# Routing steps of a fused attention and mixture-of-experts kernel put in another order, and one weight split moved by a turn

## The chip, the cores and the metric

The kernel runs on one core of one Trainium2 chip. What counts is the time of one execution on the device in microseconds (us). Before the change three runs took 968.52, 968.83 and 969.94 us; the median is 968.83 us. The engines are named as in the profile: PE is the matrix engine, DVE the vector engine, ACT the scalar engine, POOL the general engine that here also issues the scattering DMAs, and SP the engine that issues the other DMAs.

## The reference

Local attention over chunks of 64 tokens feeds a mixture of experts. Cut to what matters:

```python
# attention: 8 heads, q and k scaled inputs, chunks of 64 tokens
scores = (q_c @ k_c.T) / sqrt(64);  scores -= scores.max(-1)
attn = exp(scores);  attn /= attn.sum(-1) + 1e-9
x = (attn @ v_c)                      # to rows: 4608 tokens x 512
# gate: two of eight experts for each token
noisy = x @ w_gate + log1p(exp(x @ w_noise)) * noise
top2 = the two largest of the 8;  l = noisy[top2] - max
w = exp(l) / (sum(exp(l)) + 1e-9)
# experts: 512 -> 1024 -> 512
for e in range(8):
    for k in range(2):
        mask = top2[:, k] == e
        out[mask] += w[mask, k] * (relu(x[mask] @ w1[e]) @ w2[e])
```

## The kernel before

The 4608 tokens are 36 tiles of 128. The function `attend(it)` is one turn of a software pipeline written out by hand: in turn `it` PE computes the scores of tile it+1 (L443), the product with V of tile it-2 (`pv`, L472), the transposes of the probabilities (L460) and of the finished rows (L488). DVE takes the maxima (L448), subtracts them (L453), and in `norm_c` (L483) divides the product with V by the row sums and writes the rows x. `pv` has a single pair of PSUM banks, so `pv` of the next tile cannot begin before `norm_c` of the last one has read them. Each engine runs its instructions in program order; an instruction that waits holds up all behind it on its engine.

The rows x lie in a ring of buffers, `rows = ...tile_pool(name="rows", bufs=5)` (L339), each holding four tiles. Every fourth turn `x_next` (L438) takes the next buffer with a small memset on DVE, and that memset must wait until the rows of the group five buffers back have been scattered.

Routing runs beside the attention. After four tiles the gate matmul (L500), its transposes (L510) and a sum (L517) give the logits of a *group* of four tiles. There are seven such groups, 0 to 6, and a last one with eight tiles. The generator `route(g)` then computes, on ACT and DVE, the noisy logits (L541 to L549), the eight sorted values of each token (`MAX`, L555), the indices (L559), two one-hot tables (`goh`, L563) and their sum (`gohb`, L567). PE turns these into ranks by small matmuls (L577, L579: the *rank matmuls*). From the ranks and a running count `run` DVE makes `gr`, `gohr` and the slot numbers `lii` (L596 to L610). Beside that stand the weights of the two experts: the difference of the two maxima `gex` (L570), its exponential (L581), the sum `gsm` (L587), its reciprocal (L590) and the second weight (L607). The code of the token (L584) is written into the row.

The generator yields the name of the engine that its next step uses, and `attend` advances it at fixed places: three DVE steps after the subtraction (ahead of `norm_c`) and three after `norm_c` in each turn. A yield of "dve" costs one of these six steps; what stands between two yields goes as one step. A "pe" step is done in a fixed place in PE's row, and a "wait" holds the group until the next turn.

When a group has its slot numbers, eight scatters (four tiles, two experts each) go to a list. `scatter` takes from this list, once after the maxima and once ahead of `norm_c` in each turn: two spacing memsets (L640), a one-element copy (L642) that keeps POOL from running ahead, and an indirect DMA (L644) that writes 128 rows of x to their slots in DRAM.

Meanwhile W1 of expert 0 is split for the later three-pass matmuls: `w_split` makes a high part on ACT (L88) and a low part on POOL (L89), one half of a 128-row chunk a turn, in turns 7 to 14.

After the attention the expert blocks follow. `layer1` and `layer2` consist of matmuls at L239 from there to the end, and the rows are added into the output by indirect DMAs (L206).

Of the kernel before, what the change touches and what calls it, by code (L numbers as in the profile page):

```python
# [13 lines left out]
AF = mybir.ActivationFunctionType  # L14
# [35 lines left out]
def kernel(ctx, tc, qT, kT, vh, wgn, noise, w1, w2, out, caps=CAPS):  # L50
    nc = tc.nc
# [15 lines left out]
    def w_load(e, which, c):  # L67
        st = stage.tile([P, 1024], FT, name="st")
        staged[e, which, c] = st
        if which == 1:  # L70
            if e == 0:
                nc.sync.dma_start(st, w1[0, c * P:(c + 1) * P, :])
            else:
                for j in range(4):
                    nc.sync.dma_start(st[32 * j:32 * j + 32], w1v[ds(place[e], 1), c, j].rearrange("o r f -> (o r) f"))
        else:
            nc.sync.dma_start(st.rearrange("p (f n) -> p f n", f=2),
                              w2[ds(place[e], 1) if e else slice(0, 1), 2 * c * P:(2 * c + 2) * P, :]
                              .rearrange("o (f p) n -> p (o f) n", f=2))
# [270 lines left out]
    def load_qk(j):  # L350
        if j < NT // 2:
            QB[j] = loads.tile([P, 2, 4, P], FT, name="qb", bufs=RING)
            for h in range(2):
                nc.sync.dma_start(QB[j][h::2], qT[HALF[h], 2 * j:2 * j + 2])
                nc.sync.dma_start(KB[j % RING][h::2, h], kT[HALF[h], 2 * j:2 * j + 2])

    def load_v(j):
        if j < NT // 2:
            for h in range(2):
                nc.sync.dma_start(VB[j % RING][h::2, h], vh[HALF[h], 2 * j:2 * j + 2])  # L360
# [79 lines left out]
    def scores(t):  # L440
        for hp in range(4):
            for q in HALF:
                nc.tensor.matmul(PS[q, t % 2, hp * P:(hp + 1) * P], QB[t // 2][:, t % 2, hp, q],  # L443
                                 KB[t // 2 % RING][:, :, t % 2, hp, q], start=True, stop=True)
# [13 lines left out]
    def p_trans(t):  # L458
        for hp in range(4):
            nc.tensor.transpose(PS[:, 2, hp * P:(hp + 1) * P], PR[t][:, hp * P:(hp + 1) * P], ident)  # L460
# [37 lines left out]
    def gate_mm(g):  # L498
        for d in range(ND):
            nc.tensor.matmul(PS[32 * d:32 * d + 32, 6, :], wg[:, d, :], XT[g][:, d], start=True, stop=True)  # L500
# [19 lines left out]
    def route(g):  # L520

        V = nc.vector
# [27 lines left out]
        m = gate.tile(n8, FT, name="gm")  # L550
# [15 lines left out]
        V.memset(ohb[:, G], 0.0)  # L566
        V.tensor_add(ohb[:, 0:G], oh[:, 0], oh[:, 1])  # L567
        ex, sm = nm("gex"), nm("gsm")
        yield "dve"
        V.tensor_sub(ex, m[:, :, 1], m[:, :, 0])  # L570
        if g == LAST:
            yield "wait"
            yield "wait"
# [3 lines left out]
        nc.tensor.matmul(rk, before, ohb, start=True, stop=False)  # L577
        for k in range(1, G + 1):
            nc.tensor.matmul(rk[:, k:G + 1], ones, ohb[:, 0:G + 1 - k], start=False, stop=(k == G))  # L579
        yield "act"  # L580
        nc.scalar.activation(ex, ex, AF.Exp)  # L581
        for x, s in parts:
            yield "dve"
            V.scalar_tensor_tensor(x.bitcast(I32)[:, :, CODE], mi[:, s, 0], 8192.0, tok[:, ts][:, s], op0=OP.mult, op1=OP.add)  # L584
        yield "wait"
        yield "dve"
        V.tensor_scalar(sm, ex, 1.0, 1e-9, op0=OP.add, op1=OP.add)  # L587
# [6 lines left out]
        yield "dve"  # L594
        r8 = n3("gr8")
        V.scalar_tensor_tensor(r8, rk[:, 0:G], 8.0, be(run8), op0=OP.mult, op1=OP.add)  # L596
        yield "dve"
        V.scalar_tensor_tensor(run8, rk[:, G], 8.0, run8, op0=OP.mult, op1=OP.add)
        yield "dve"
        ohr = gate.tile([P, 2, G, NE], FT, name="gohr")  # L600
# [65 lines left out]
    def load_early():  # L666
        for i, js, m in early:
            gather(i)
            early_loads.append(nc.sync.dma_start(
                meta0[i], by_slot[js * P:(js + m) * P, 0, CODE:USED].rearrange("(j p) c -> p j c", p=P)))  # L670
        early.clear()
# [28 lines left out]
    def next_turn():  # L700
        for r in routing:
            if r[1] == "wait":
                r[1] = next(r[0])
# [22 lines left out]
    def attend(it):  # L726
        STEPS = 6
        if it % 2:
            load_qk((it - 1) // 2 + 3)
        if it % 2 == 0 and it >= 4:  # L730
            load_v((it - 4) // 2 + 3)
            if it == 32:
                load_early()
        if it in (9, 11):
            for r in range(CLEAN + 64 * (it // 2 - 4), CLEAN + 64 * (it // 2 - 3), 16):
                nc.sync.dma_start(slots[r * NE:(r + 16) * NE, 0:USED], zero)
        if it == 11:
            nc.sync.dma_start(slots[(CLEAN + P) * NE:NLIST * P * NE, CODE:USED].rearrange("(p r) c -> p r c", p=P),
                              zero[:, 0:3 * (NLIST * P - CLEAN - P) // 16].rearrange("p (r c) -> p r c", c=3))
        if it in range(4, 8):  # L740
            w_load(0, 1, it - 4)
        if it in (29, 31, 33, 35):
            w_load(0, 2, (it - 29) // 2)
        next_turn()
        if it == 0:
            scores(0)
        if it <= 1:
            p_trans(0) if it else scores(1)
        if it == 2:
            pv(0)  # L750
        if 0 < it < NT - 1:
            scores(it + 1)
        if 0 < it - 2 < NT:
            pv(it - 2)
        gated = it - 4 >= 0 and (it - 4) % 4 == 3
        if gated:
            gate_mm((it - 4) // 4)
        if 0 < it - 1 < NT:
            p_trans(it - 1)
        if 0 <= it - 3 < NT:  # L760
            x_trans(it - 3)
        if it - 5 >= 0 and (it - 5) % 4 == 3:
            gate_turn((it - 5) // 4)
            if grp_of[it - 5] != grp_of.get(it - 4):
                r = route(grp_of[it - 5])
                routing.append([r, next(r)])
        step_route("pe")
        if 0 <= it - 2 < NT:
            norm_a(it - 2)
        if 0 <= it - 1 < NT:  # L770
            p_copy(it - 1)
        if it < NT:
            mx = soft_max(it)
            soft_sub(it, mx)
            scatter(1, mx[0:1, 0, 0:1])
            soft_exp(it)
        if 0 <= it - 3 < NT:
            x_copy(it - 3)
        if gated:
            gate_copy((it - 4) // 4)  # L780
        step_route("dve", STEPS // 2)
        if 0 <= it - 2 < NT:
            norm_b(it - 2)
            scatter(1, RC[it - 2][0:1, 0, 0])
            norm_c(it - 2)
        if it - 5 >= 0 and (it - 5) % 4 == 3:
            gate_sum((it - 5) // 4)
        step_route("act")
        step_route("dve", STEPS // 2)
        if it >= 1 and (it - 1) % 4 == 0:  # L790
            x_next((it - 1) // 4)
        if it in range(33, 38):
            zero_out(3)
        if it == NT + 2:
            scatter(2, XT[(it - 3) // 4][0:1, 0, (it - 3) % 4, 0:1])
        elif it == NT + 3:
            scatter(2, LS[(it - 4) // 4][0:1, 0, 0:1])
        if it in range(7, 15):
            w_split(0, 1, *wq.pop(0), eng=nc.gpsimd)

    for it in range(NT):
# [242 lines left out]
```

## Time and profile before

| | |
|---|---|
| median of three runs | 968.83 us |
| profiled execution | 974.74 us |
| its span in the trace | 972.9 us |
| PE busy | 951.2 us, 98% |
| DVE busy | 457.5 us, 47% |
| ACT busy | 287.3 us, 30% |
| POOL busy | 236.3 us, 24% |

A row of a timeline gives start, duration, engine, line, operation, output<-input and, in brackets, how long the engine sat idle before it and what ended that idle time. Runs of equal instructions are one row with a count (x16). A row of windows gives, for a stretch of time, the busy time and the number of instructions of PE, PE's weight loads, DVE, ACT and POOL, then the granted clock of PE (1.00 is full), the share of the DMA engines that was busy, and GB/s.

The turns are easily found in the trace: each begins on DVE with L448. Turn 13 begins at 50.10 us, turn 14 at 53.37, turn 26 at 94.31, turn 30 at 110.13. The expert blocks begin at 137.53 us.

### The profile page before, as it was taken

To read this page: it belongs to the slowest core of one execution; us is meant where nothing else is said; L and a number is where in the kernel's file an instruction comes from. 1 tells how busy PE (TensorE), PEld (TensorE's weight loads), DVE (VectorE), ACT (ScalarE), POOL (GpSimd) and SP (SyncE) were. 2 spreads that over 40 slices of the span, in tenths; PEclk is the share of its full clock that TensorE was granted. 3 is DMA by queue.
4 is the path that set the end of the run, shared out by engine and by line. 5 is a ranking of instruction groups with operands and counts; after the bars stand their busy time and mean duration, and the time that the engine had idled before them with its cause. 6 is when DMAs were issued, how large, how long until landed. Compare 5 with 4: busy or idle time off the path is not lost. (4 is left out here: it accounts for less than half of the span.)

```text
span 972.9 us, 16180 instructions
## 1 busy us (share of the span) xinstructions
PE 951.2 (98%) x5776; PEld 846.5 (87%) x5776; DVE 457.5 (47%) x1026; ACT 287.3 (30%) x623; POOL 236.3 (24%) x426
## 2 busy tenths in 40 slices
PE   7999899999999999999999999999999999999996
PEld 6788678888897999899898989889998999899886
DVE  6798767226253542463255425443444343434311
ACT  3767553114141321241132214121312231223100
POOL 3267768430202011101111111211011011111113
PEclk9999999999999999999999999999999999999999
DMA  8999996987604632265316521652174217312213
GB/s 301 379 354 376 342 355 222 367 136 153 166 14 98 188 60 32 44 172 116 44 34 155 141 44 33 145 140 44 25 165 126 54 23 162 109 14 31 33 22 45
DMA packets 97300, 132.94 MB, mean 137 GB/s; under 512 B 23456, under 2 KB 56864, under 8 KB 97216
## 3 DMA queue, kind: packets, MB, share of 16 engines
q1 hardware_dynamic: 80160, 92.50, 31.0%
q0 software_dynamic: 16576, 38.33, 19.9%
q10 hardware_dynamic: 480, 1.05, 0.4%
q8 instruction: 46, 0.75, 0.3%
q14 instruction: 38, 0.31, 0.1%
HBM read 81.69 MB, written 50.13 MB: 135 GB/s over the span
## 5 line engine op out<-in xcount | busy, mean ns | idle before, releaser
L206 POOL DMA_INDIRECT out<-o,lid x75 | 116.7, 1557 | 647.2 <-DVE o L274 625.9
L239 PE MATMUL PS<-xh,w1h 128*128 128x384 f32 (+2 forms) x768 | 261.7, 341 | 1.9 <-issue 1.9
L239 PE MATMUL PS<-xl,w1h 128*128 128x384 f32 (+2 forms) x768 | 260.9, 340 | 0.2 <-issue 0.2
L239 PE MATMUL PS<-xh,w1l 128*128 128x384 f32 (+2 forms) x768 | 260.7, 339 | 0.0
L258 ACT ACTIVATE hh<-PS 128x384 fp32r<-128x384 f32 (+2 forms) x192 | 95.2, 496 | 463.0 <-PE PS L239 418.0
L239 PE MATMUL PS<-w2h,hh 128*128 128x512 f32 (+1 forms) x592 | 229.3, 387 | 0.0
L239 PE MATMUL PS<-w2h,hl 128*128 128x512 f32 (+1 forms) x592 | 229.1, 387 | 0.0
L239 PE MATMUL PS<-w2l,hh 128*128 128x512 f32 (+1 forms) x592 | 229.0, 387 | 0.0
L261 DVE SCALAR_TENSOR_TENSOR hl<-PS,hh 128x384 fp32r<-128x384 f32 (+2 forms) x192 | 108.6, 566 | 175.1 <-ACT hh L258 135.6
L274 DVE TENSOR_SCALAR o<-PS,lwt 128x512 f32<-128x512 f32 (+2 forms) x73 | 54.7, 749 | 224.8 <-PE PS L239 217.5
L239 PEld LDWEIGHTS PS<-xh,w1h 128*128 128x128 f32 x768 | 144.6, 188 | 8.2 <-issue 6.5
L239 PEld LDWEIGHTS PS<-xl,w1h 128*128 128x128 f32 x768 | 144.6, 188 | 2.1 <-issue 0.5
L239 PEld LDWEIGHTS PS<-xh,w1l 128*128 128x128 f32 x768 | 144.7, 188 | 1.0
L239 PEld LDWEIGHTS PS<-w2h,hl 128*128 128x128 f32 x592 | 110.8, 187 | 23.1
L239 PEld LDWEIGHTS PS<-w2l,hh 128*128 128x128 f32 x592 | 110.8, 187 | 22.2
L239 PEld LDWEIGHTS PS<-w2h,hh 128*128 128x128 f32 x592 | 110.8, 187 | 22.2
L644 POOL DMA_INDIRECT slots<-xs,lii x72 | 71.2, 989 | 26.0 <-issue 23.9
L229 ACT ACTIVATE xh<-y 128x512 fp32r<-128x512 f32 x67 | 41.2, 614 | 92.4 <-DVE y L226 90.4
L230 DVE TENSOR_TENSOR xl<-y,xh 128x512 fp32r<-128x512 f32 x67 | 44.9, 671 | 48.0 <-ACT xh L229 45.9
L443 PE MATMUL PS<-kb,qb 128*64 128x128 f32 x576 | 42.0, 291 | 9.1 <-DMA kb<-in_kT 7.1
L203 POOL MEMSET spacer<- 1x1 f32 x78 | 47.7, 612 | 0.0
L226 DVE STREAM_TRANSPOSE y<-xg 128x512 f32<-128x512 f32 x67 | 45.6, 680 | 0.0
(131 smaller groups left out, 692.8 us busy)
## 6 DMA issues: line engine op xcount, KB each, us to landing
st<-in_w SPq DMA_DIRECT2D x36, 512.0 KB
xg<-slots SPq DMA_DIRECT2D x252, 64.0 KB
st<-in_w SPq DMA_DIRECT2D x112, 128.0 KB
out<-zero SPq DMA_DIRECT2D x37, 256.0 KB
vb<-in_vh SPq DMA_DIRECT2D x36, 260.0 KB
qb<-in_qT SPq DMA_DIRECT2D x34, 256.0 KB
kb<-in_kT SPq DMA_DIRECT2D x32, 256.0 KB
xg<-slots SPq DMA_DIRECT2D x9, 256.0 KB
```

The source lines that it names most:

```text
L203: nc.gpsimd.memset(spacer, 0.0)
L206: s = nc.gpsimd.indirect_dma_start(out=to, out_offset=bass.IndirectOffsetOnAxis(ap=at[0:r], axis=0), in_=o, in_offset=None, compute_op=OP.add)
L226: nc.vector.transpose(y[:, 0:4 * r], x[:, 0:4 * r])
L229: nc.scalar.activation(oh, src, AF.Copy)
L230: nc.vector.tensor_sub(ol, src, oh.bitcast(FT))
L239: nc.tensor.matmul(p, a, b, start=first and n == 0, stop=last and n == 2)
L258: nc.scalar.activation(hh[:, 0:n], p, AF.Relu)
L261: nc.vector.scalar_tensor_tensor(hl[:, 0:n], p, 0.0, hh[:, 0:n].bitcast(FT), op0=OP.max, op1=OP.subtract)
L274: nc.vector.tensor_scalar(o[0:r], p[0:r], w, None, op0=OP.mult)
L443: nc.tensor.matmul(PS[q, t % 2, hp * P:(hp + 1) * P], QB[t // 2][:, t % 2, hp, q], KB[t // 2 % RING][:, :, t % 2, hp, q], start=True, stop ...
L644: s = nc.gpsimd.indirect_dma_start(out=slots, out_offset=bass.IndirectOffsetOnAxis(ap=lii[:, k, t0 + r:t0 + r + 1], axis=0), in_=XS[(t0 + ...
```

## The change

In `route` the difference of the maxima goes from ahead of the rank matmuls to behind them. The code of the token comes ahead of the exponential and not behind it. Two "dve" yields go away with that: the one in front of the difference (the difference now has the yield behind the rank matmuls) and the one between the two updates at `gr` and `run`. The splits of W1 of expert 0 are done in turns 6 to 13 in place of 7 to 14.

```diff
@@ in route
         ex, sm = nm("gex"), nm("gsm")
-        yield "dve"
-        V.tensor_sub(ex, m[:, :, 1], m[:, :, 0])
         if g == LAST:
             yield "wait"
...
             nc.tensor.matmul(rk[:, k:G + 1], ones, ohb[:, 0:G + 1 - k], start=False, stop=(k == G))
-        yield "act"
-        nc.scalar.activation(ex, ex, AF.Exp)
+        yield "dve"
+        V.tensor_sub(ex, m[:, :, 1], m[:, :, 0])
         for x, s in parts:
             yield "dve"
             V.scalar_tensor_tensor(x.bitcast(I32)[:, :, CODE], mi[:, s, 0], 8192.0, tok[:, ts][:, s], op0=OP.mult, op1=OP.add)
+        yield "act"
+        nc.scalar.activation(ex, ex, AF.Exp)
         yield "wait"
...
         V.scalar_tensor_tensor(r8, rk[:, 0:G], 8.0, be(run8), op0=OP.mult, op1=OP.add)
-        yield "dve"
         V.scalar_tensor_tensor(run8, rk[:, G], 8.0, run8, op0=OP.mult, op1=OP.add)
@@ in attend
-        if it in range(7, 15):
+        if it in range(6, 14):
             w_split(0, 1, *wq.pop(0), eng=nc.gpsimd)
```

Because the steps are dealt out six to a turn, this moves work by whole turns. Group 0 has its slot numbers in turn 12 where it had them in turn 14; groups 1 to 6 have them three turns sooner. Three places show it.

The first is DVE in turn 26, from the maxima L448 to the end of the turn. Before:

```order
L448 TENSOR_REDUCE mx<-PS 128x8
L453 TENSOR_TENSOR pr<-PS,mx 128x4x2x64
L587 TENSOR_SCALAR gsm<-gex 128x4
L590 RECIPROCAL xs<-gsm 128x4
L596 SCALAR_TENSOR_TENSOR gr_1611<-PS,run_159 128x32
L480 RECIPROCAL rc<-rc 128x8
L483 TENSOR_TENSOR xs<-PS,rc 128x512
L598 SCALAR_TENSOR_TENSOR run_159<-PS,run_159 128x8
L601 TENSOR_TENSOR gohr<-goh,gr_1611 128x64
L604 COPY lim_87<-run_159 128x1
L607 TENSOR_TENSOR xs<-gex,xs 128x4
```

The same turn of the changed kernel, where the line numbers are lower by one or two from L571 of before on:

```order
L448 TENSOR_REDUCE mx<-PS 128x8
L453 TENSOR_TENSOR pr<-PS,mx 128x4x2x64
L555 MAX gm<-gsp 128x8 x2
L559 MAX_INDEX gmi<-gm,gsp 128x8 x4
L480 RECIPROCAL rc<-rc 128x8
L483 TENSOR_TENSOR xs<-PS,rc 128x512
L563 TENSOR_TENSOR goh<-e_row,gmi 128x32 x2
L566 MEMSET gohb 128x4
L567 TENSOR_TENSOR gohb<-goh 128x32
```

Ahead of `norm_c` (L483) stood the sum, the reciprocal and `gr` of group 3; there stand now two `MAX` and four index searches of group 4. Group 3's tail has gone to turn 24. Turns 14, 18, 22, 30 and 34 end up with the same rows as turn 26. The turn behind each of these is lighter than before: it held `lii` and four `MAX` ahead of `norm_c` and now holds the difference and the code.

The second place is POOL where the splits of W1 end and the scatters begin. Before:

```order
L89 TENSOR_TENSOR w1l_706<-st,w1h_705 128x512 x2
L89 TENSOR_TENSOR w1l_821<-st,w1h_820 128x512
L640 MEMSET spacer 1x1 x2
L642 COPY spacer<-rc 1x1
L644 DMA slots<-xs,lii 44032x576
L89 TENSOR_TENSOR w1l_821<-st,w1h_820 128x512
L640 MEMSET spacer 1x1 x2
L642 COPY spacer<-mx 1x1
L644 DMA slots<-xs,lii 44032x576
```

Now:

```order
L89 TENSOR_TENSOR w1l_652<-st,w1h_651 128x512 x2
L89 TENSOR_TENSOR w1l_779<-st,w1h_778 128x512
L639 MEMSET spacer 1x1 x2
L641 COPY spacer<-mx 1x1
L643 DMA slots<-xs,lii 44032x576
L639 MEMSET spacer 1x1 x2
L641 COPY spacer<-rc 1x1
L643 DMA slots<-xs,lii 44032x576
L89 TENSOR_TENSOR w1l_779<-st,w1h_778 128x512
```

Two scatters where there was one now stand ahead of the last low part of W1, and the first one follows the maxima of turn 13 where it followed the row sums of turn 14.

The third place is DVE around the last but one `norm_c`, where the first expert block is being prepared: `xl` (L230) is the low part of a tile of x for that block, which has three such tiles. Before:

```order
L230 TENSOR_TENSOR xl_2200<-PS,xh_2199 128x4x128
L563 TENSOR_TENSOR goh<-e_row,gmi 128x32
L566 MEMSET gohb 128x4
L567 TENSOR_TENSOR gohb<-goh 128x32
L570 TENSOR_TENSOR gex<-gm 128x4
L480 RECIPROCAL rc<-rc 128x8
L483 TENSOR_TENSOR xs<-PS,rc 128x512
L517 TENSOR_REDUCE lg<-PS 128x64
L230 TENSOR_TENSOR xl_2200<-PS,xh_2199 128x4x128 x2
```

Now:

```order
L230 TENSOR_TENSOR xl_2234<-PS,xh_2233 128x4x128
L587 TENSOR_SCALAR gsm<-gex 128x4
L590 RECIPROCAL xs<-gsm 128x4
L596 SCALAR_TENSOR_TENSOR gr_2287<-PS,run_159 128x32
L597 SCALAR_TENSOR_TENSOR run_159<-PS,run_159 128x8
L480 RECIPROCAL rc<-rc 128x8
L483 TENSOR_TENSOR xs<-PS,rc 128x512
L517 TENSOR_REDUCE lg<-PS 128x64
L600 TENSOR_TENSOR gohr<-goh,gr_2287 128x64
L603 COPY lim_88<-run_159 128x1
L606 TENSOR_TENSOR xs<-gex,xs 128x4
L609 TENSOR_REDUCE lii<-gohr 128x2x4
```

The two `xl` of the block's later tiles now follow directly behind the last row shown, so group 6's slot numbers stand ahead of them.

## The prediction, made before the result was known

> **What bounds the kernel now.** I read the page's busy table first, then windows of the attention and of the expert blocks, then the timeline where a window has a hole in it. The page's chain of waits ends in the last scatter into the output and says nothing of this change.
>
> ```profile
> PE 951.2 (98%) x5776; PEld 846.5 (87%) x5776; DVE 457.5 (47%) x1026; ACT 287.3 (30%) x623; POOL 236.3 (24%) x426
> ```
>
> PE is busy 951.2 of 972.9 us, so all that any edit can win without touching PE's own work is some 21.7 us of idle time and the time PE spends at a lowered clock. Where are these? The windows give, behind the stretch and its length, busy time and count of PE, its weight loads, DVE, ACT and POOL, then the granted clock, the share of the DMA engines and GB/s.
>
> ```profile
> 80.00:100.00 20.00, 20.00 (x269) 16.51 (x265) 18.04 (x73) 12.51 (x32) 14.12 (x41) 1.00 1.01 378
> 100.00:120.00 20.00, 17.49 (x214) 13.80 (x213) 14.73 (x65) 10.96 (x27) 13.97 (x44) 0.91 0.96 355
> 112.00:114.00 2.00, 1.47 (x24) 1.25 (x22) 1.86 (x7) 0.69 (x2) 1.43 (x5) 0.86 1.03 406
> 114.00:116.00 2.00, 2.00 (x18) 0.86 (x15) 1.54 (x8) 0.27 (x1) 1.37 (x5) 0.50 0.82 321
> 116.00:118.00 2.00, 2.00 (x18) 0.97 (x12) 1.93 (x12) 0.39 (x1) 1.34 (x4) 0.78 1.01 321
> 600.00:800.00 200.00, 200.00 (x1025) 181.22 (x1024) 85.57 (x138) 50.27 (x98) 30.26 (x38) 1.00 0.42 90
> ```
>
> The steady attention (80 to 100 us) keeps PE at 20.00 of 20.00 at full clock, with DVE close behind at 18.04. The expert blocks, of which 600 to 800 us stands for the rest, keep PE full with every other engine under half: what leaves the attention early arrives early at the end, one for one. The hole lies in 100 to 120 us: PE misses 2.51 us, and its clock is 0.91. The fine windows place the lowered clock: 0.86, 0.50, 0.78 in 112 to 118 us.
>
> In the timeline (start, duration, engine, line; in brackets the idle time before and what ended it) the hole has one cause:
>
> ```profile
> 103.08 0.98 POOL L644 DMA_INDIRECT slots<-xs,lii  x1 [0.42 <-issue]
> 107.24 0.19 DVE L549 TENSOR_TENSOR gsp<-gsp,lg 128x32 f32<-128x32 f32 x1
> 110.13 0.06 DVE L438 MEMSET xs<- 128x1 f32 x1 [2.69 <-DMA slots<-xs,lii]
> 110.13 0.69 DVE L448 TENSOR_REDUCE mx<-PS 128x8 f32<-128x512 f32 x1
> 111.60 1.09 PE L443 MATMUL PS<-kb,qb 128*64 128x128 f32 x16 [1.98 <-DVE pr L453]
> 113.23 1.83 PE L472 MATMUL PS<-vb,pts 128*64 128x130 f32 x16 [0.54 <-DVE xs L483]
> ```
>
> At the end of turn 29 DVE wants the ring buffer of rows that group 2 had, and stands 2.69 us until the last of group 2's scatters has landed, the 24th of all, issued at 103.08: 7.05 us from issue to release. The maxima of turn 30 are behind that memset, and PE's scores wait 1.98 us for them. Then the same 16 matmuls of `pv` take 1.83 us and not 1.06 (the row at 97.20 below).
>
> Why was that scatter late? POOL is the pace:
>
> ```profile
> 54.49 1.27 POOL L89 TENSOR_TENSOR w1l<-st,w1h 128x512 fp32r<-128x512 f32 x1 [1.21 <-ACT w1h L88]
> 56.30 0.18 POOL L642 COPY spacer<-rc 1x1 f32<-1x1 f32 x1 [0.36 <-DVE rc L480]
> 57.42 1.17 POOL L644 DMA_INDIRECT slots<-xs,lii  x1 [0.95 <-DMA qb<-in_qT]
> 58.63 1.28 POOL L89 TENSOR_TENSOR w1l<-st,w1h 128x512 fp32r<-128x512 f32 x1
> 62.12 0.24 POOL L642 COPY spacer<-rc 1x1 f32<-1x1 f32 x1
> 101.17 0.98 POOL L644 DMA_INDIRECT slots<-xs,lii  x1 [0.44 <-issue]
> ```
>
> The last two scatters of group 2 were issued at 101.17 and 103.08, 1.91 us apart, with a short issue gap and no wait on a gate. Eight at that pace take 15.2 us; a group of four turns takes less (turn 26 began at 94.31, turn 30 would have begun at 107.43 without the wait: 13.1). POOL falls further behind in each group until the ring runs out, so where it starts, it stays ahead: a scatter that starts so much sooner at 62 us is so much sooner at 103.
>
> **The change, part by part.**
>
> *Scatters start sooner: the wait goes.* In the changed order two scatters stand ahead of the last low part of W1, where one stood. That last low part is now a turn sooner, too, and its predecessor takes the place of the low part seen here before it:
>
> ```profile
> 52.01 1.27 POOL L89 TENSOR_TENSOR w1l<-st,w1h 128x512 fp32r<-128x512 f32 x1 [2.10 <-ACT w1h L88]
> 53.78 0.63 ACT L88 ACTIVATE w1h<-st 128x512 fp32r<-128x512 f32 x1
> ```
>
> I build POOL's new row from these: the low part of 52.01 ends at 53.28; memsets and copy to 53.8 (group 0 has its slot numbers in turn 12, and the gate, the maxima of turn 13, is long past); first DMA 54.1 to 55.3; second copy at 55.6, its DMA to 57.2; the last low part (its high part is ready at 54.4) to 58.5; third copy 58.8. Before it was at 62.12: a lead of 3.3 us. The first scatter's DMA sat 0.95 us where later ones sit 0.44; if the first one again needs that, the lead is 2.8. I take 3.0, with 3.3 and 2.3 (the same 0.5 once more, should the zeros that are written to its slots land late) as bounds. The 24th scatter then goes out at 103.08 - 3.0 = 100.1 and, with the same 7.05 us, releases the buffer at 107.1. DVE wants it at 107.43. So the wait goes whole: **-2.7**. With a lead of 2.3 some 0.4 of it stays; DVE's own delays below ask for the buffer 0.75 later by then, which covers that.
>
> *The clock.* In 112 to 118 us PE lost 2 x 0.14 + 2 x 0.50 + 2 x 0.22 = 1.7 us to the lowered clock. It is lowered only here and behind another hole (below), and full where PE runs without one. Without the hole I count it as gone: **-1.7** (bounds 0 and -1.7). [...]
>
> *Routing on DVE, another order.* No instruction goes away, so DVE's sum per group stays. What counts is what stands ahead of `norm_c` (L483), since PE's next `pv` waits for it. Turns 18, 22, 26, 30 and 34 had the sum, reciprocal and `gr` there; they get two `MAX` and four searches. The old row is in turn 26, the new one in turn 10 of this same trace:
>
> ```profile
> 95.64 0.16 DVE L587 TENSOR_SCALAR gsm<-gex 128x4 f32<-128x4 f32 x1
> 96.00 0.19 DVE L480 RECIPROCAL rc<-rc 128x8 f32<-128x8 f32 x1
> 96.30 0.69 DVE L483 TENSOR_TENSOR xs<-PS,rc 128x512 f32<-128x512 f32 x1
> 97.20 1.06 PE L472 MATMUL PS<-vb,pts 128*64 128x130 f32 x16
> ```
>
> ```profile
> 41.34 0.23 DVE L555 MAX8 gm<-gsp 128x8 f32<-128x8 f32 x2
> 42.03 0.18 DVE L480 RECIPROCAL rc<-rc 128x8 f32<-128x8 f32 x1
> 42.31 0.69 DVE L483 TENSOR_TENSOR xs<-PS,rc 128x512 f32<-128x512 f32 x1
> 43.15 1.11 PE L472 MATMUL PS<-vb,pts 128*64 128x130 f32 x16 [0.41 <-DVE xs L483]
> ```
>
> Old: 96.00 - 95.64 = 0.36 us. New: 42.03 - 41.34 = 0.69. `norm_c` ends 0.33 later; it ended at 96.99 and `pv` began at 97.20, so 0.21 of that is hidden by PE's scores and 0.12 shows. In turn 10, with the new row, PE waited 0.41. I take 0.25 a turn, about halfway between the two, times five: **+1.25** (0 to 2.05). Lower is possible since the turn behind is relieved: its `lii` and four `MAX` ahead of `norm_c` go. Turn 14 has the new row as well, but there PE has waits enough; I count nothing.
>
> *The second ring wait.* The next memset, four turns on, needs the 32nd scatter. It found its buffer free:
>
> ```profile
> 118.29 0.98 POOL L644 DMA_INDIRECT slots<-xs,lii  x1 [0.44 <-issue]
> 125.48 0.06 DVE L438 MEMSET xs<- 128x1 f32 x1 [0.21 <-DMA slots<-xs,lii]
> ```
>
> DVE comes 2.7 + 1.7 - 1.0 = 3.4 sooner, at 122.0; the scatter 3.0 sooner, at 115.3. With 7.05 us again it would land at 122.3: a wait of 0.3. The bound from this row itself is 125.48 - 118.29 = 7.2. I take **+0.1** (0 to 0.5).
>
> *The end of attention.* The two last `xl` now stand behind `gohr`, `lim`, the weight and `lii` of group 6.
>
> ```profile
> 96.98 0.21 DVE L601 TENSOR_TENSOR gohr<-goh,gr 128x64 f32<-128x64 f32 x1
> 97.25 0.68 DVE L448 TENSOR_REDUCE mx<-PS 128x8 f32<-128x512 f32 x1
> ...
> 135.97 1.28 DVE L230 TENSOR_TENSOR xl<-PS,xh 128x512 fp32r<-128x512 f32 x2
> 137.53 0.42 PE L239 MATMUL PS<-xh,w1h 128*128 128x384 f32 x1
> 137.78 0.34 PE L239 MATMUL PS<-xl,w1h 128*128 128x384 f32 x1
> ```
>
> In turn 26 `gohr`, `lim` and the weight take 0.27 us (96.98 to the next turn's 97.25); with about half of that again for `lii`, some 0.4, so `xl` ends at 137.65 in place of 137.25, where PE wants it at 137.78 less the rank matmuls that no longer precede it (0.13). I take **+0.3** (0 to 0.7, if what is ahead of the `norm_c` there grows as well).
>
> *At nothing:* the earlier splits, which lie on ACT and POOL in this stage,
>
> ```profile
> 20.00:40.00 20.00, 20.00 (x272) 16.95 (x270) 14.34 (x33) 14.36 (x34) 2.56 (x2) 1.00 1.01 384
> ```
>
> with ACT at 14.36 and POOL at 2.56 of 20 beside a full PE; and the exponential behind the code, on an ACT at 12.51 of 20. Uncovered, one high part on ACT's way is 0.63.
>
> Sum: -2.7 - 1.7 + 1.25 + 0.1 + 0.3 = -2.75. The span goes from 972.9 to about 970.15, the profiled execution from 974.74 to 972.0. The median of the plain runs is 5.9 us below the profiled one; I carry the difference over to it: 968.83 - 2.75 = **966.1 us**.
>
> **The rivals.**
>
> *No change.* The lowered clock does not go with the hole, but falls a little later: PE still idles 1.01 us for `norm_c` near 128 us. Then the sum is -1.05: **967.8**. [...] Or the plain runs, 5.9 us shorter, never had this wait; then only the costs are left, +1.65: 970.5. For it: the runs differ by that much and I see only one. Against: the stall is made by POOL's pace, which does not depend on a profile.
>
> *Slower: `norm_c` becomes the bound.* The whole new row (0.69) and the pair of `MAX` that now ends the turn ahead of it (0.23) fall on PE in each of six turns, turn 14 among them: 6 x 0.92 = 5.5. PE then idles often enough that the lowered clock stays. 5.5 + 0.1 + 0.3 - 2.7 = +3.2: **972.0**. It decides from 0.71 a turn on (6 x 0.71 + 0.4 - 2.7 = 1.9). For it: DVE at 18.04 of 20, and the 0.41 of turn 10. Against: the slack of 0.21, and DVE's unchanged sum.
>
> *More gain.* A second hole stands behind the first block:
>
> ```profile
> 176.61 0.41 PE L239 MATMUL PS<-xh,w1h 128*128 128x384 f32 x1 [1.91 <-issue]
> ```
>
> ```profile
> 178.00:180.00 2.00, 2.00 (x9) 2.00 (x8) 0.75 (x1) 0.00 (x0) 0.00 (x0) 0.58 1.04 388
> 180.00:182.00 2.00, 2.00 (x8) 2.00 (x8) 0.56 (x1) 0.49 (x1) 0.56 (x2) 0.57 1.03 386
> ```
>
> PE stands about 2.3 us in all and then loses 2 x 0.42 + 2 x 0.43 = 1.7 to the clock, with the DMA engines at 1.04. The loads of that block follow group 6's last scatter, which comes sooner. If that removes the hole, 4.0 more: **962.1**. Against it: the row names no release by such a load.
>
> **How the numbers follow.** The forecast has 0.40, no change 0.25, slower 0.18, more gain 0.17. About 0.2% (1.9 us) is what a measurement of this kernel can tell from no change. The forecast with its unknown costs runs from 964.5 to 967.9, three quarters of it below 966.9: faster 0.30, same 0.10. No change gives 0.20 to same, 0.03 to faster, 0.02 to slower. Slower gives 0.16 and 0.02 to same; more gain 0.15 and 0.02 to same. Together faster 0.48, same 0.34, slower 0.18. The range reaches from the price of more gain to the middle of slower: 962.2 to 971.0.
>
> **What will show it.** Right: the memset at L438 of turn 29 has no wait on a scatter; the third scatter's copy is at about 59; windows around 112 to 118 us show a clock of 1.00 and PE full. Wrong in the scatter's lead: the 24th scatter is issued later than 101. Wrong in DVE's order: rows at L472 in turns 18 to 34 with an idle of over 0.5 released by L483, and groups that take longer than 13.4 us. The end: first matmul of the expert blocks at about 134.8 (137.53 - 2.75). Wrong altogether: the clock falls elsewhere in the attention, or the hole at 176 grows.

## The result, and the profile after

The changed kernel takes 974.69 us (median of five runs, 974.01 to 975.43) against 969.94 us for the kernel before (five runs, 968.52 to 970.80). The ratio is 1.0052, with an interval of 1.0037 to 1.0066: slower by about 5 us. I had forecast 966.1 us, within 962.2 to 971.0, and given "slower" a chance of 0.18.

The page of the changed kernel, its busy table:

```profile
span 973.1 us, 16186 instructions
PE 948.3 (97%) x5776; PEld 843.5 (87%) x5776; DVE 459.3 (47%) x1026; ACT 288.0 (30%) x623; POOL 236.3 (24%) x431
```

PE is busy 2.9 us less than before in a span that is 0.2 us longer. The windows of the changed kernel answer those of the prediction (length; busy time of PE, weight loads, DVE, ACT, POOL; clock; DMA share; GB/s):

```profile
80.00:100.00 20.00, 19.41 (x259) 16.31 (x257) 17.48 (x75) 12.97 (x35) 14.35 (x42) 1.00 1.00 362
100.00:120.00 20.00, 18.81 (x248) 14.98 (x246) 16.82 (x63) 11.58 (x29) 13.78 (x44) 1.00 1.00 368
140.00:160.00 20.00, 17.51 (x111) 15.84 (x110) 11.67 (x54) 8.88 (x21) 15.96 (x39) 1.00 0.97 366
600.00:800.00 200.00, 200.00 (x1025) 181.22 (x1024) 85.47 (x139) 50.28 (x98) 30.27 (x38) 1.00 0.43 90
```

The hole in 100 to 120 us is smaller (18.81 in place of 17.49) and the clock there is full, as forecast. But 80 to 100 us, where PE was full, now lacks 0.59 us, and 140 to 160 us, also full before, lacks 2.49. Later on, in 600 to 800 us, PE and its weight loads are the same to the digit (200.00 and 181.22).

What I had set out to remove is gone. The memset of turn 29 and the scatter that it needs, in the timeline of the changed kernel:

```profile
100.92 0.98 POOL L643 DMA_INDIRECT slots<-xs,lii  x1 [0.44 <-issue]
112.23 0.06 DVE L438 MEMSET xs<- 128x1 f32 x1 [0.17 <-DMA slots<-xs,lii]
```

The 24th scatter goes out at 100.92 (103.08 before) and DVE waits 0.17 and not 2.69 us. What came in its place stands in PE's rows:

```profile
55.17 1.11 PE L472 MATMUL PS<-vb,pts 128*64 128x130 f32 x16 [0.87 <-ACT w1h L88]
85.14 1.09 PE L443 MATMUL PS<-kb,qb 128*64 128x128 f32 x16
86.82 1.11 PE L472 MATMUL PS<-vb,pts 128*64 128x130 f32 x16 [0.58 <-DVE xs L483]
100.98 1.11 PE L472 MATMUL PS<-vb,pts 128*64 128x130 f32 x16 [0.58 <-DVE xs L483]
115.38 1.11 PE L472 MATMUL PS<-vb,pts 128*64 128x130 f32 x16 [0.58 <-DVE xs L483]
129.52 1.11 PE L472 MATMUL PS<-vb,pts 128*64 128x130 f32 x16 [1.67 <-DVE xs L483]
133.36 0.66 PE L222 MATMUL PS<-ident,xg 128*128 128x128 f32 x4 [0.61 <-DMA xg<-slots]
138.77 0.42 PE L239 MATMUL PS<-xh,w1h 128*128 128x384 f32 x1
146.79 0.66 PE L510 MATMUL PS<-ident,ls 128*128 128x128 f32 x4 [1.69 <-ACT ls L504]
155.53 0.19 PE L575 MATMUL PS<-gohb,before 128*128 128x72 bf16 x1 [0.80 <-DVE gohb L567]
```

There are two kinds. Once in each group, in turns 22, 26, 30 and 34, `pv` waits for `norm_c`. And at and behind the end of attention PE waits for the rows of the first expert block, for the gate's copy, and for the last group's routing. The first matmul of the expert blocks comes at 138.77, where I had forecast 134.8.

Why is `norm_c` late? DVE rows of the changed kernel from `norm_c` of turn 24 to that of turn 26, some left out:

```profile
92.70 0.69 DVE L483 TENSOR_TENSOR xs<-PS,rc 128x512 f32<-128x512 f32 x1
93.46 0.42 DVE L517 TENSOR_REDUCE lg<-PS 128x64 f32<-128x256 f32 x1
93.80 0.21 DVE L600 TENSOR_TENSOR gohr<-goh,gr 128x64 f32<-128x64 f32 x1
94.20 0.68 DVE L448 TENSOR_REDUCE mx<-PS 128x8 f32<-128x512 f32 x1
97.42 0.24 DVE L555 MAX8 gm<-gsp 128x8 f32<-128x8 f32 x2
97.83 0.69 DVE L448 TENSOR_REDUCE mx<-PS 128x8 f32<-128x512 f32 x1 [0.17 <-DMA slots<-xs,lii]
99.17 0.23 DVE L555 MAX8 gm<-gsp 128x8 f32<-128x8 f32 x2
100.14 0.69 DVE L483 TENSOR_TENSOR xs<-PS,rc 128x512 f32<-128x512 f32 x1
```

From 92.70 on DVE has no gap over 0.17 us until `norm_c` of turn 26, which begins at 100.14: 7.44 us from the one to the other. In the second profile of the old kernel (below) it is 6.87 us (89.81 to 96.68), with gaps of 0.15 and 0.36 in it. Three pieces of work are new in this stretch: the tail of the old group from `gohr` to `lii`, 0.40 us (93.80 to 94.20); a pair of `MAX` in turn 25 where the token's code stood; and in turn 26 `MAX` and searches, 0.68 (99.17 to 99.85), where the sum and `gr` took 0.36. The theory with which I went into the experiments was therefore: **A**, DVE is crowded between `norm_c` of turn 4n and of turn 4n+2. Its rivals were the splits of W1, and a wait of DVE for the exponential:

```profile
91.82 0.17 DVE L587 TENSOR_SCALAR gsm<-gex 128x4 f32<-128x4 f32 x1 [1.02 <-ACT gex L584]
```

### The profile page after: what moved, and what is told of

Same layout as the page of the kernel before. It is cut to its first block, busy times and chain, and to the rows that moved or that the text cites. A ratio compares the mean times of both kernels' runs of the same rounds, so it can differ in the third digit from the quotient of the medians.

```text
span 973.1 us, 16186 instructions
## 1 busy us (share of the span) xinstructions
PE 948.3 (97%) x5776; PEld 843.5 (87%) x5776; DVE 459.3 (47%) x1026; ACT 288.0 (30%) x623; POOL 236.3 (24%) x431
## 5 line engine op out<-in xcount | busy, mean ns | idle before, releaser
L206 POOL DMA_INDIRECT out<-o,lid x75 | 116.8, 1557 | 647.6 <-DVE o L274 626.4
L230 DVE TENSOR_TENSOR xl<-y,xh 128x512 fp32r<-128x512 f32 x67 | 44.9, 671 | 47.9 <-ACT xh L229 47.9
L89 DVE TENSOR_TENSOR w2l<-st,w2h 128x512 fp32r<-128x512 f32 x64 | 44.3, 692 | 2.9 <-DMA out<-zero 2.9
```

The costliest lines, as they stand in the source:

```text
L89: (eng or nc.vector).tensor_sub(lo[:, s], st[:, s], hi[:, s].bitcast(FT))
L206: s = nc.gpsimd.indirect_dma_start(out=to, out_offset=bass.IndirectOffsetOnAxis(ap=at[0:r], axis=0), in_=o, in_offset=None, compute_op=OP.add)
L230: nc.vector.tensor_sub(ol, src, oh.bitcast(FT))
```

## Experiments: the parts apart, and what the old wait was worth

All ratios are to the kernel before, run on the same chip beside each of the three sets: 970.1, 969.75 and 969.32 us.

**The kernel before once more.** No edit.

> The kernel before, unchanged, for a second profile and the granted clock of each execution. If the wait of 2.69 us at the ring of rows and the two stretches of half clock belong to every execution, the clock is again 0.995 and the wait stands in the new profile. If they came only in the profiled execution that was shown (974.7 us against a median near 970), the clock is about 0.998 and the memset of turn 29 waits less than 0.5 us.

Measured: 969.12 us, ratio 0.9997 (0.9987 to 1.0006); span 966.9 us, clock 0.997. Two windows, `norm_c` of turns 24 and 26, and the memset of this second profile of the old kernel:

```profile
104.00:120.00 16.00, 14.51 (x196) 12.16 (x197) 13.06 (x51) 9.88 (x26) 11.44 (x35) 1.00 0.94 348
174.00:182.00 8.00, 8.00 (x48) 8.00 (x47) 1.96 (x4) 1.96 (x4) 6.05 (x15) 1.00 1.03 382
```

```profile
89.81 0.69 DVE L483 TENSOR_TENSOR xs<-PS,rc 128x512 f32<-128x512 f32 x1
96.68 0.69 DVE L483 TENSOR_TENSOR xs<-PS,rc 128x512 f32<-128x512 f32 x1
109.48 0.06 DVE L438 MEMSET xs<- 128x1 f32 x1 [1.75 <-DMA slots<-xs,lii]
```

The answer lies between the two expectations: the ring wait belongs to the old kernel, at 1.75 us here, but neither stretch of half clock is there, and the second hole at 176 us is gone. The execution from which I forecast lost 3.4 us to the lowered clock (1.7 us in each of two places) and had a hole of 2 us that this one does not have. The clock of each timed run says that the lowered clock is no accident of one execution: of the 50 runs of the old kernel beside the three sets, 12 have a mean clock of 0.995 or less and take 971.3 us on average, and 19 have 0.998 or more and take 968.7.

**The routing order alone.**

```diff
 (the changed kernel)
-        if it in range(6, 14):
+        if it in range(7, 15):
```

> The routing order of the change alone, the splits of W1 in turns 7 to 14 as before. Theory: the new order crowds DVE's work between norm_c of turn 4n and norm_c of turn 4n+2, about 0.8 us a group that PE waits for, so this kernel alone is slower than before by 4 to 5 us (ratio about 1.0045). Rival: the loss comes from the splits that meet the routing steps in turns 12 to 14; then this kernel is within 1.5 us of before.

Measured: 975.94 us, ratio 1.0064 (1.0051 to 1.0076). The loss is the routing order's.

**The splits alone.**

```diff
 (the kernel before)
-        if it in range(7, 15):
+        if it in range(6, 14):
```

> The splits of W1 in turns 6 to 13 alone, the routing order as before. Theory: within 1 us of before, since PE's waits in the groups from turn 16 on do not depend on it. Rival (the splits carry the loss): slower by 3 us or more.

Measured: 967.80 us, ratio 0.9974 (0.9965 to 0.9984): faster by about 2.5 us, which neither theory had. The two profiles differ by 0.6 us only (spans 966.3 and 966.9), and the first expert block begins at 134.94 and 135.04. A part of the rest stands in the clocks: all nine runs have a mean clock of 0.997 or more, while 6 of the 21 runs of the old kernel beside them have 0.995; the 7 of these with 0.998 or more take 969.0 us on average, which leaves 1.2 us. Why the earlier splits should keep the clock up, no run here shows.

**The ring wait alone.**

```diff
 (the kernel before, in scatter)
-            for _ in range(2 if attending[0] else 1):
+            for _ in range(1):
                 nc.gpsimd.memset(spacer, 0.0)
```

> Before with one spacing memset a scatter in place of two, which makes POOL's pace 1.76 in place of 1.91 us and brings the 24th scatter some 3 us sooner, with DVE's order untouched. If the ring wait and the half clock behind it are in the timed runs: faster by 2.7 to 4.4 us. If they are not: within 1 us of before.

Measured: 966.08 us, ratio 0.9959 (0.9946 to 0.9972), span 964.2: 4.0 us faster, inside the 2.7 to 4.4 expected. From the maxima of turn 28 to those of turn 30 it takes 6.91 us (100.52 to 107.43 below), where the second profile of before has 8.44 (101.04 to 109.48): 1.5 us of the gain is the ring wait. The forecast's idea, that POOL's pace feeds a wait in the attention, holds.

```profile
100.52 0.68 DVE L448 TENSOR_REDUCE mx<-PS 128x8 f32<-128x512 f32 x1
107.43 0.06 DVE L438 MEMSET xs<- 128x1 f32 x1 [0.21 <-DMA slots<-xs,lii]
```

How the other 2.5 us divide is not shown. The two spans differ by 2.7 us only (966.9 and 964.2), 0.7 of it behind turn 35, and the clock of the five runs is 0.997 to 0.999, so the lowered clock in a part of the old kernel's runs is a likely share of the 4.0.

## Experiments: what the new order costs

**The searches behind `norm_c`.**

```diff
 (the changed kernel, in attend: ahead of norm_c, and behind it)
-        step_route("dve", STEPS // 2)
+        step_route("dve", 1 if it % 4 == 2 else STEPS // 2)
...
-        step_route("dve", STEPS // 2)
+        step_route("dve", 5 if it % 4 == 2 else STEPS // 2)
```

> The changed kernel with the four index searches of each group moved from ahead of norm_c to behind it in turns 14, 18, 22 and so on (one step ahead, five behind, in place of three and three). Theory (DVE is crowded between norm_c of turn 4n and of turn 4n+2): the searches take 0.55 us there (85.14 to 85.69), so PE's wait at L472 falls from 0.58 to 0.2 or less in each of six groups, and the time by about 3 us, to 971 or 972. Rival (DVE's wait of 1.02 us for the exponential in turn 4n carries the loss): nothing moved ahead of or behind the exponential, so 974 to 975.5.

Measured: 974.34 us, ratio 1.0046 (1.0029 to 1.0064). By the time alone theory A has failed. The profile says otherwise. Turn 24 and turn 28 of this kernel begin at

```profile
88.43 0.68 DVE L448 TENSOR_REDUCE mx<-PS 128x8 f32<-128x512 f32 x1
102.04 0.68 DVE L448 TENSOR_REDUCE mx<-PS 128x8 f32<-128x512 f32 x1
126.31 1.11 PE L472 MATMUL PS<-vb,pts 128*64 128x130 f32 x16 [1.13 <-DVE xs L483]
133.05 0.73 PE L222 MATMUL PS<-ident,xg 128*128 128x128 f32 x4 [3.51 <-DMA xg<-slots]
```

A group takes 13.61 us where the changed kernel takes 14.16 (89.40 to 103.56): 0.55 less, as expected from the 0.55 us of searches, and the waits at L472 between turns 16 and 33 are gone. But PE then stands 3.51 us for the rows of the first expert block, which cost 0.61 in the changed kernel, and behind that wait its clock falls (0.94 from 130 to 134 us, 0.64 from 134 to 138), which loses another 1.7 us. Most of what was won is given back. So there is a second cause, and it sits at the end of the attention.

**Without the exponential.** The exponential of the difference is left out (its two lines), so the weights of the experts are other numbers.

> The changed kernel with the exponential of the difference left out (the weights of the two experts are then other numbers; the slots are the same). Theory: the 1.02 us wait of DVE for ACT in turn 4n goes, but norm_c of that turn waits for PE's pv anyway (ACT's copy of the row sums starts at 92.06, norm_c at 92.70), so the time stays within 1 us of the changed kernel, 974 to 975.5. Rival (the wait for the exponential carries the loss): 4 us or more faster, about 970.

Measured: 975.26 us, ratio 1.0055 (1.0035 to 1.0075). The wait for the exponential carries nothing that can be seen in the time: as computed beforehand, `norm_c` of that turn could not have come sooner. DVE now waits 0.99 us at the reciprocal of the row sums instead, and a group takes 14.18 us.

**The tail of the group elsewhere.**

```diff
 (the changed kernel, in route; "..." are lines left out)
         yield "act"
         nc.scalar.activation(ex, ex, AF.Exp)
-        yield "wait"
-        yield "dve"
-        V.tensor_scalar(sm, ex, 1.0, 1e-9, op0=OP.add, op1=OP.add)
-        for x, s in parts:
-            yield "dve"
-            V.reciprocal(x[:, :, WA], sm[:, s])
...      (gr, run, gohr)
+        yield "dve"
+        with nc.allow_low_precision(reason="one whole number below 2**24 among zeros"):
+            V.tensor_reduce(lii[:, :, ts], ohr, AX.X, OP.add)
+        yield "wait"
+        yield "dve"
+        V.tensor_scalar(sm, ex, 1.0, 1e-9, op0=OP.add, op1=OP.add)
+        for x, s in parts:
+            yield "dve"
+            V.reciprocal(x[:, :, WA], sm[:, s])
...      (the second weight)
-        yield "dve"
-        with nc.allow_low_precision(reason="one whole number below 2**24 among zeros"):
-            V.tensor_reduce(lii[:, :, ts], ohr, AX.X, OP.add)
```

The wait for the next turn now stands behind the slot numbers and not ahead of `gr`, so a group also has its slot numbers a turn sooner.

> The changed kernel with gr, run, gohr and the slot numbers of a group moved from turn 4n to the second half of turn 4n+3, ahead of the sum and the weights, which stay in turn 4n. Theory: 0.40 us (93.80 to 94.20) leaves the crowded stretch behind norm_c of turn 4n, six groups, so 2 to 2.5 us faster than the changed kernel, about 972.3, with PE's wait at L472 in turns 4n+2 near 0.2. Rival (only what stands right ahead of norm_c in turn 4n+2 counts, the searches and MAX): 974 to 975.5.

Measured: 979.10 us, ratio 1.0090 (1.0072 to 1.0109): slower than any other, not faster. In the steady groups it did as A says, in part: a group takes 13.83 us (from 88.32 to 102.15 below, 14.16 before) and the wait is 0.33.

```profile
58.34 1.09 PE L443 MATMUL PS<-kb,qb 128*64 128x128 f32 x16 [1.79 <-DVE pr L453]
88.32 1.11 PE L472 MATMUL PS<-vb,pts 128*64 128x130 f32 x16 [0.34 <-DVE xs L483]
102.15 1.11 PE L472 MATMUL PS<-vb,pts 128*64 128x130 f32 x16 [0.33 <-DVE xs L483]
135.39 0.66 PE L222 MATMUL PS<-ident,xg 128*128 128x128 f32 x4 [2.35 <-DMA xg<-slots]
```

It lost at the start of the scatters (1.79) and, again, at the rows of the first block (2.35). The 1.79 goes back to a product of routing on DVE that took 2.22 us (0.18 at its median in the changed kernel), with a low part of W1 on POOL in the same stretch:

```profile
54.23 2.22 DVE L547 TENSOR_TENSOR gsp<-gsp,nz 128x32 f32<-128x32 f32 x1
55.12 1.27 POOL L89 TENSOR_TENSOR w1l<-st,w1h 128x512 fp32r<-128x512 f32 x1
```

The profiled run is the fastest of its six (976.88), with a clock of 0.998; the other five have 0.992 to 0.995, so lowered clock is a part of the median that this profile does not show.

## Experiments: POOL's backlog at the end

What is late there? SP's load of the first block's rows and, 15 to 18 us later, ACT's first high part of W2. Before:

```profile
122.97 1.32 SPq L171 DMA_DIRECT2D xg<-slots  x3
138.83 0.18 POOL L642 COPY spacer<-rc 1x1 f32<-1x1 f32 x1 [0.86 <-DVE rc L480]
141.22 0.63 ACT L88 ACTIVATE w2h<-st 128x512 fp32r<-128x512 f32 x1
```

Changed:

```profile
130.34 1.31 SPq L171 DMA_DIRECT2D xg<-slots  x3
145.41 0.18 POOL L641 COPY spacer<-rc 1x1 f32<-1x1 f32 x1
145.62 0.63 ACT L88 ACTIVATE w2h<-st 128x512 fp32r<-128x512 f32 x1 [2.82 <-POOL spacer L641]
```

The load stands at a fixed place in the program, at the start of turn 32, and must wait for all scatters that stand ahead of it. In the old kernel the last of these is the 33rd of the list, issued at 120.20; in the changed one it is the 38th, issued at 127.57, because the list is filled sooner. In both the load goes out 2.77 us behind that issue. W2's tile lies in memory that the attention's small tiles leave, so its first write waits for the last POOL copy that reads one of them: that copy belongs to the 43rd scatter before and to the 48th now. Before, it was done at 139.01, 2.2 us ahead of the write; now the write follows it at once. In both places the program asks POOL for five scatters more at the same point, and POOL does one in 1.9 us. Five of them are 9.5 us; the lead of 2.2 us pays for less than a quarter. Theory **B** is the late load, theory **C** the late copy.

**The late load put into the old kernel.**

```diff
 (the kernel before, in attend)
-            if it == 32:
+            if it == 34:
                 load_early()
```

> The kernel before, with the load of block 0's rows put in turn 34 in place of 32, so that it stands behind the 37th scatter of the list and not the 33rd; the routing order is that of before. Theory B (the changed kernel issues this load five scatters later because its list is ahead of POOL): four scatters at 1.9 us make the load 7 us later (130 in place of 123), PE waits 2 us or more for it at L222, and the time is 2 to 3.5 us over before. Rival (the load has slack enough, the loss in the changed kernel is DVE's order alone): within 1 us of before.

Measured: 972.98 us, ratio 1.0037 (1.0023 to 1.0050), the size that B expects, but not by B alone:

```profile
128.26 1.11 PE L472 MATMUL PS<-vb,pts 128*64 128x130 f32 x16 [2.87 <-DVE xs L483]
134.30 0.66 PE L222 MATMUL PS<-ident,xg 128*128 128x128 f32 x4 [1.31 <-DMA xg<-slots]
```

The load is issued at 131.22, again 2.76 us behind the issue of the last scatter ahead of it, the 37th (128.46), and PE waits 1.31 us for it. The 2.87 at 128 us goes back to a second ring wait: the memset at 125.43 waits 2.23 us for a scatter, where the second profile of before has none (turn 33 to 34 takes 5.63 us), and the clock falls behind it (0.91 from 126 to 130 us, 0.66 from 130 to 134). It came with the move of the load, perhaps because three writes of zeros that stood behind the load on SP's queue (126.82 in that profile) now go out at 116.57, ahead of that scatter; no run tests this. So the run shows that the load has no slack for such a delay; it does not give B's price.

**The early load put sooner, with the searches behind `norm_c`.**

```diff
 (the changed kernel with the searches behind norm_c)
-            if it == 32:
+            if it == 30:
                 load_early()
```

> The changed kernel with the index searches behind norm_c (as in c1) and the load of block 0 in turn 30, behind the 34th scatter and not the 38th. Theory B alone: PE's wait of 3.51 us at L222 goes and the time falls to about 971. Theory C (the first high part of W2 waits for a POOL copy that stands behind the 48th scatter, at 145.4 in the changed kernel and 138.8 before): PE arrives sooner and waits for that copy in place of the load, by L510, so 973 to 974.5. Rival, neither: 974.3 with the same waits.

Measured: 974.69 us, ratio 1.0057 (1.0043 to 1.0071). The load goes out at 122.64, 2.79 us behind the 34th scatter (119.85), and the wait of 3.51 is gone. The loads of V behind it on SP's queue now wait in turn, 3.60 us at PE, and W2 waits for POOL all the same:

```profile
133.48 1.11 PE L472 MATMUL PS<-vb,pts 128*64 128x130 f32 x16 [3.60 <-DMA vb<-in_vh]
145.49 0.63 ACT L88 ACTIVATE w2h<-st 128x512 fp32r<-128x512 f32 x1 [1.73 <-POOL spacer L641]
146.66 0.66 PE L510 MATMUL PS<-ident,ls 128*128 128x128 f32 x4 [0.60 <-ACT ls L504]
```

The expectation that B alone would not pay held; that the wait would move to V's loads I had not seen.

**A faster POOL under the changed order.** The edit of the ring experiment (one spacing memset) made in the changed kernel.

> The changed kernel with one spacing memset a scatter, so that POOL does a scatter in 1.76 and not 1.91 us; DVE's order is that of the change. Theories B and C: the load of block 0 is issued near 126.7 and the POOL copy that W2 waits for comes near 140, so the waits of 0.61 at L222 and 1.69 at L510 go: about 972. DVE's crowding stays, with 0.58 at L472 in each group and groups of 14.1 us, so it stays above before. Rival (the loss at the end has nothing to do with POOL's backlog): 974 to 975.5.

Measured: 972.79 us, ratio 1.0034 (1.0021 to 1.0047). The load goes out at 123.26, W2's first part at 142.31 without a wait, and the waits at L222 and L510 are not there any more. The waits of 0.58 at L472 are, and so is the one for the last group's routing at L575 (0.73).

**Both causes taken away.** The same edit made in the kernel with the searches behind `norm_c`.

> The changed kernel with the index searches behind norm_c and one spacing memset a scatter: both causes taken away. Theory (crowded DVE, and POOL's backlog at the end): the 0.54 us a group that c1 won in the attention and lost at the end now stays won, so about 3 us below the kernel with one spacing memset alone, 968 to 969, near or below before. Rival (the two overlap): no better than that kernel, 972.

Measured: 969.63 us, ratio 1.0003 (0.9994 to 1.0011): the 0.55 us a group that the searches won and lost again is now kept, 3.2 us below the kernel ahead. That is level with the kernel before, but not all of the loss: beside the old order with the same POOL (966.08, in another set) 3.5 us remain. Turns 12 to 35 are 2.5 us longer (80.62 against 78.09 us in the table below), and 0.8 of that is made up by the first matmul of the expert blocks (8.37 us later against 9.13). What makes up the rest is not taken apart.

**The two gains on the old order.** Splits a turn sooner and one spacing memset, routing as before.

> The routing order of before, the splits of W1 a turn sooner, and one spacing memset a scatter. If the two gains are separate they add: 970.1 x 0.9959 x 0.9974 = 963.6. If both come from the ring of rows they don't: 966.

Measured: 965.64 us, ratio 0.9952 (0.9933 to 0.9971). They do not add. This is the fastest of all kernels here, below both that were given, though not clearly below the one spacing memset alone (966.08).

## Why the prediction was wrong, point by point

The profiles put the loss in two places, the attention and its end. The table gives, in us, the stretch from the maxima of turn 12 to those of turn 35, and from there to the end, from the turn starts and spans of each profile.

| kernel | turn 12 to 35 | turn 35 to the end |
|---|---|---|
| before, second profile | 79.74 | 841.01 |
| before, one spacing memset | 78.09 | 840.35 |
| changed | 83.41 | 843.38 |
| changed, searches behind `norm_c` | 80.45 | 845.52 |
| changed, one spacing memset | 83.44 | 841.29 |
| changed, both | 80.62 | 840.73 |

- **Scatters start sooner: right, and nearly of the size.** The third copy came at 59.90, where I had 58.8 to 59.3; the 24th scatter at 100.92 where I had 100.1; the lead was 2.2 us, just outside my bounds of 2.3 to 3.3. The ring wait went.
- **Its worth: too high by the second profile, not refuted by the times.** I priced it at 2.7 us and the lowered clock behind it at 1.7. Both came from one execution. In the second profile of the old kernel the wait is 1.75 us with no stretch of half clock behind it; taken away alone it is worth 1.5 us there. But one spacing memset, which takes this wait away and leaves DVE's order, won 4.0 us by the medians, some of it behind the attention, and lowered clock does stand in a part of the old kernel's runs. The five runs of the changed kernel have 0.998 to 0.999. So the 4.4 may have been nearly won; it is the costs that were too small. (That the plain runs, 5.9 us shorter than the profiled one, might lack the wait I had named, but only as a part of a rival.)
- **Routing on DVE: the step that failed.** I counted what stands ahead of `norm_c` in one turn, 0.33 us less 0.21 of slack, and took 0.25 a group, 1.25 in all. What sets `norm_c` of turn 4n+2 is all of DVE's work since `norm_c` of turn 4n: 0.40 of the old group's tail and a pair of `MAX` in place of a code came into this stretch as well. PE's `pv` began 1.68 us after its scores (85.14 to 86.82) where it took 0.92 before: 0.76 a group. Over turns 12 to 35 it is 83.41 - 78.09 = 5.3 us against the old order without a ring wait. A part of this depends on where the stretch ends. In the new order the last turn of a group is short (turn 27 takes 2.39 us, 3.40 in the old order with one memset), and the stretch ends ahead of the last turn of its last group: over whole groups, turns 12 to 32, it is 71.64 - 68.22 = 3.4 us. But that last short turn gave nothing back; from turn 35 to the first matmul of the expert blocks the two take 9.05 and 9.13 us. I had written that DVE's sum per group stays, so that only the one place counts; the sum stays, but a group's work was bunched in two turns, with the last turn almost empty.
- **The turns at the start.** I counted nothing for turns 12 to 16. They took 16.04 us (46.31 to 62.35) where the second profile of before has 15.12 (46.15 to 61.27): 0.9 of the 5.3. A subtraction of routing took 1.29 us (0.19 at its median) beside a low part of W1 on POOL that ran from 52.60 on, and `norm_c` stood behind it. The old order has one such meeting (0.99 at L541, 54.82 in its first profile, beside a low part from 54.49 on; 0.98 in its second), the new one a second at 58.56, where a pair at L563 took 1.27 and not 0.28, beside a low part from 58.38 on:

```profile
52.64 1.29 DVE L543 TENSOR_TENSOR gsp<-gsp,gu 128x32 f32<-128x32 f32 x1
52.60 1.27 POOL L89 TENSOR_TENSOR w1l<-st,w1h 128x512 fp32r<-128x512 f32 x1 [2.03 <-ACT w1h L88]
```

- **The end of attention: wrong in kind, the second step that failed.** I priced the two `xl` at 0.3, though my own rows had them end just when PE wanted them (137.65, and 137.78 less 0.13), and counted nothing for the transfers that wait for scatters. The real cost is 843.38 - 841.01 = 2.4 us, most of it by POOL's backlog: a list filled three turns sooner puts more scatters ahead of everything that waits for "all scatters so far", and POOL's pace did not change. One spacing memset takes 2.1 of it away (843.38 to 841.29). The 0.80 at L575, where PE waits for the last group's tables, is not POOL's: with one memset 0.73 of it stays.
- **At nothing: the splits.** Alone they are not a loss, but a gain of 2.5 us, for about half of which the clocks account; the rest I cannot place.
- **The rivals.** "Slower: `norm_c` becomes the bound" is what happened in the attention, down to the sign that I had named for it (idle over 0.5 at L472, released by L483, groups over 13.4 us), at 0.76 a group where I had 0.92. That lowered clock would stay was wrong; the backlog took its place. "More gain" rested on the second hole, put at 2.3 us where its rows add up to 2.13; the second profile of before does not have it. The forecast's own span is a little off, too: with its bounds it runs from 964.4 to 967.7, not from 964.5 to 967.9.

In sum, by the table: 1.65 won at the ring (79.74 - 78.09, if one spacing memset does nothing else there), 5.32 lost to DVE's order (0.9 of it at the start) and 2.37 at the end, mostly to the backlog. Taken together that is 6.0 of the 6.2 us between the two spans (966.9 and 973.1).

## What to carry to other kernels

When steps are moved between turns, add up all the work of that engine between two points at which another engine needs it, not only what stands right ahead of the second point. A list that is filled sooner while its worker keeps its pace is a longer backlog for everything that stands at a fixed place in the program and waits for "all so far": ask which loads and which reused buffers those are. And size a stall on more than one execution, above all where the profiled time and the median differ by more than the effect.

## What was not expected of the hardware

- In the first profile of before the granted clock was 0.50 from 113.6 to 116.8 us and from 178.4 to 181.6, behind PE waits of 1.98 us (ended at 111.60) and 1.91 us (ended at 176.61): about 3.4 us each time, with the edges. Windows of 4 us show it lowered behind waits of 2.87 us (the late load: 0.91 and 0.66 from 126 to 134), 3.51 us (searches behind `norm_c`: 0.94 and 0.64 from 130 to 138) and 3.60 us (the early load: 0.59 and 0.98 from 134 to 142), a loss of 1.7 us in each. It was not lowered behind one of 2.35 us (tail elsewhere; clock 1.00 from 130 to 150 us) or of 1.69 us (changed; 1.00 from 140 to 160). So in these profiles the length of the wait alone does not decide it. The windows behind the waits, in the order searches, early load, tail elsewhere:

```profile
134.00:138.00 4.00, 4.00 (x32) 3.66 (x31) 2.27 (x8) 1.85 (x4) 2.76 (x10) 0.64 1.02 353
134.00:138.00 4.00, 4.00 (x29) 3.83 (x25) 1.68 (x7) 1.46 (x3) 2.87 (x10) 0.59 1.05 408
134.00:138.00 4.00, 2.61 (x29) 2.27 (x30) 1.22 (x5) 1.93 (x6) 2.87 (x9) 1.00 0.95 305
```

- A DVE operation of 0.19 us (L543 of the changed kernel) took 1.29 us beside a POOL subtraction of 1.27 us, and one of 0.18 (L547) took 2.22 us in the kernel with the tail elsewhere, with such a subtraction of 1.27 us in the same stretch. The first cost here because it stood ahead of `norm_c` (at 54.37), the second because the next turn's maxima stood behind it (at 56.87).
